# Attention with decay feeding a squared-ReLU MLP in float32: one head pair divided on chip, two more unsplit heads, a third bank, squares on ScalarE

## The chip, the cores and the metric

The kernel runs on one core of a Trainium2 chip. The metric is device time in microseconds (us), the median of repeated executions. The profile is that of a single execution, in which every instruction of the engines has its own record: TensorE (PE, with PEld for its weight loads), VectorE (DVE), ScalarE (ACT), GpSimd (POOL), and SyncE (SP), which here issues most of the DMAs.

## The reference, cut to what matters

```python
# q, k, v: (8, 8, 576, 64), f: (8, 8, 576): 8 batches of 8 heads
scores = scale * q @ k.T
cum = cumsum(log(clip(f, 1e-4, 1.0)), axis=-1)
scores = where(causal, -1e9, scores + cum[..., :, None] - cum[..., None, :])
attn = exp(scores - max(scores))
attn = attn / (sum(attn) + 1e-9)
x = (attn @ v) -> 4608 tokens x 512
h = maximum(x @ w_in, 0.0)          # w_in: 512 x 2048
out = (h * h @ w_out)               # w_out: 2048 x 512
```

The inputs of attention are float32, and w_in and w_out are float64, which the kernel turns to float32 itself, from the two 32-bit words of each number.

## The kernel before, in words

**Heads and slots.** The 64 heads run one after the other, and each is six score units (UNITS), a block of up to 128 keys by a stretch of queries: 320, 320, 192, 64, 448 and 256 queries in this order, the last for the first key block. One unit is one slot, so head h has slots 6h to 6h + 5. In slot n the program writes down, engine by engine: the score products of unit n, the product with v for the unit of two slots earlier (LAG), the steps of a division that are due, the maxima of the next head, preparation and loads of later heads, weight conversion, and steps of the MLP. `in_order` (L18) then keeps each of PE, ACT, DVE and POOL in the order in which this was traced, so a waiting instruction holds all behind it on its engine.

**Precision, and two kinds of head.** Float32 products on PE take two instruction records each and more time than single ones in the rounded type (float32r). Heads below NWHOLE are "unsplit": `score` (L392) and `av_part` (L456) multiply float32 operands as they are, a mask is added in PSUM by a product with the constant mz (L395), and the row of maxima is turned by small products with an identity (`turn_maxima`, L377, L381) and enters the score product as an extra row. From NWHOLE on heads are "split": q, k, v and the probabilities are divided into a rounded high and a low part (`prep` L313 to L324, `split_v` L332 and L333, `split_p` L424 and L425), the products are taken in the rounded type (L399, L402; L435 to L437), POOL masks the probabilities (L411), and the maxima reach the operand by five small DMAs (L359).

**Maxima.** `max_units` (L339): for each stretch of queries one rounded product (L346) into a PSUM bank, then a reduction on DVE (L354) that reads it. The banks come in turn from banks["m"], 4 and 5, until the MLP starts; from then on "m" is empty and the maxima take the score banks, "s". These are 1, 2, 3, then 1, 2, 3, 5 while chunk 0 runs, and 1 and 2 alone from chunk 1's start to chunk 2's.

**Division.** Two heads share a tile of x (heads on partitions 0 to 63 and 64 to 127) and a tile den with the sums of the probabilities, one row a head (L471). `finish` divides a pair in four parts, in batch 0 in the slots 2, 5, 8 and 11 after the pair's last: part 0 sends both rows by DMA into a 128 x 9 tile (L481), part 1 adds epsilon and inverts on DVE (L483, L484) and sends the result to DRAM (L486), part 2 broadcasts it back over 64 partitions each (L489, two DMAs), part 3 multiplies on POOL (L492).

**Weights.** Sixteen pairs of 128 x 512 blocks are converted during the first 97 slots or so by `weight_ops`, a row of 132 small steps on DVE (L228, L233, L236, L240), ACT (L205, L210) and POOL (L216), some per slot by RATES: 1 at first, then 1.6, then 0.8 up to ready[0], then 2.

**MLP.** 18 chunks of 256 tokens by 16 blocks of the hidden layer. Each (chunk, block) is two half-steps: `mlp1`, twelve products (L522) with the two parts of x (`split_x`, L509 and L510) and of the weights, a ReLU (L530), the float32 square g on DVE (L531), the rounded square gh on ACT (L532) and their difference gl on DVE (L533); and `mlp2`, one step behind, six products (L545). A batch's chunks are started when its last pair is divided: ready[0] is slot 60, and `fill` spreads 64 half-steps, chunks 0 and 1, evenly up to ready[1], slot 104. While weights are still being converted, chunk 0 takes a block as soon as its weights are there, and chunk 1 goes on where chunk 0 has to wait (`next_step`).

## Time and profile before

| | |
|---|---|
| median of 3 runs | 1232.01 us (1229.84 to 1234.22) |
| the profiled execution | 1229.0 us |
| its span, first to last instruction | 1227.3 us |
| granted TensorE clock, mean | 0.989 |
| busy PE, PEld, DVE, ACT, POOL | 97%, 85%, 64%, 58%, 31% |

The rows below come from one execution. A group's row has line, engine, operation, tiles and shapes, the count, then busy time and mean of one in ns, and the idle time of the engine just before, with what ended it. A wait's row has who waited for whom, us in total, how often, and the longest. A stage's row has its start and end, its length, busy time (and count) of the engines named, the granted clock, the DMA engines' mean busy share and what they moved. A timeline row has start, length, engine, line and operation. The end of a matmul is modelled, so successive matmuls overlap in the records, and the distance between starts says more than a duration.

### The profile page before, as it was taken

What the parts mean: (1) busy time and instruction counts of PE and PEld (TensorE: products, weight loads), DVE (VectorE), ACT (ScalarE), POOL (GpSimd) and SP (SyncE); (2) the same over time, 40 slices, a digit from 0 to 9 for tenths busy, and PEclk for the clock granted to TensorE, in tenths of its full rate; (3) what the DMA queues carried; (4) which work ended last, traced back from release to release, by engine and by line L of the source; (5) the groups of instructions that cost most, each with busy time, mean ns of one, the idle gap of its engine ahead of it and who ended that gap; (6) DMA issues with size and microseconds to landing.
All of it is one profiled execution on the core that took longest, in us unless ns stands there. A gap on an engine that the chain in (4) does not pass through costs nothing.

```text
span 1227.3 us, 23243 instructions
## 1 busy us (share of the span) xinstructions
PE 1187.9 (97%) x7770; PEld 1047.9 (85%) x7770; DVE 781.5 (64%) x2046; ACT 710.3 (58%) x1748; POOL 376.4 (31%) x566
## 2 busy tenths in 40 slices
PE   6997998899999999999999999999999999999998
PEld 3665877788999899999999989998999899999997
DVE  5767778876666767666665666767666667533322
ACT  2774655556666666665656666666666666533232
POOL 3332234533333333332322243333333433200000
PEclk8998999899999999999999999999999999999999
DMA  7777501121221212111111121211111212000000
GB/s 216 209 187 178 185 16 33 25 70 34 48 50 41 59 41 53 37 44 36 49 19 56 26 59 42 58 41 45 38 52 41 59 41 59 11 28 1 18 18 18
DMA packets 106376, 71.88 MB, mean 59 GB/s; under 512 B 88184, under 2 KB 88184, under 8 KB 106256
## 3 DMA queue, kind: packets, MB, share of 16 engines
q1 hardware_dynamic: 105136, 66.26, 21.0%
q0 software_dynamic: 1120, 4.13, 1.4%
q8 instruction: 62, 1.02, 0.4%
q14 instruction: 58, 0.48, 0.1%
HBM read 60.20 MB, written 9.88 MB: 57 GB/s over the span
## 4 chain that ended last, share of the span: by engine, by line
PE 76%; ACT 2%; issue 2%; POOL 1%; DVE 0%; DVEq 0%; POOLq 0%
PE bank L522 30%; PE bank L545 28%; PE bank L435 3%; PE bank L437 3%; PE bank L402 3%; PE bank L436 3%; PE bank L346 3%; PE bank L399 3%; POOL v L333 0%; ACT den L471 0%; ACT p L409 0%; ACT r L530 0%; ACT ph L424 0%; ACT gh L532 0%; POOL p L411 0%
## 5 line engine op out<-in xcount | busy, mean ns | idle before, releaser
L545 PE MATMUL bank<-w,gh 128*128 128x512 f32 x1152 | 412.9, 399 | 0.0
L522 PE MATMUL bank<-xh,w 128*128 128x256 f32 x2304 | 331.5, 287 | 5.5 <-DVE tcol L354 5.5
L522 PEld LDWEIGHTS bank<-xh,w 128*128 128x128 f32 x2304 | 303.5, 191 | 13.2 <-DVE tcol L354 5.9
L425 DVE TENSOR_TENSOR pl<-p,ph 128x320 fp32r<-128x320 f32 (+4 forms) x300 | 186.0, 620 | 196.9 <-ACT ph L424 191.4
L545 PEld LDWEIGHTS bank<-w,gh 128*128 128x128 f32 x1152 | 217.1, 188 | 38.1
L530 ACT ACTIVATE r<-bank 128x256 f32<-128x256 f32 x288 | 110.3, 383 | 220.3 <-PE bank L522 200.3
L545 PE MATMUL bank<-w,gl 128*128 128x512 f32 x576 | 226.8, 394 | 0.1
L531 DVE TENSOR_TENSOR g<-r 128x256 f32<-128x256 f32 x288 | 128.5, 446 | 139.0 <-ACT r L530 138.3
L411 POOL TENSOR_SCALAR_AFFINE_SELECT p<-p 128x128 f32<-128x128 f32 (+1 forms) x250 | 83.6, 334 | 423.6 <-ACT p L409 322.7
L424 ACT CAST ph<-p 128x320 fp32r<-128x320 f32 (+4 forms) x300 | 124.4, 415 | 152.3 <-POOL p L411 110.2
L522 PE MATMUL bank<-xl,w 128*128 128x256 f32 x1152 | 185.6, 284 | 0.0
L522 PEld LDWEIGHTS bank<-xl,w 128*128 128x128 f32 x1152 | 159.3, 192 | 0.0
L533 DVE TENSOR_TENSOR gl<-g,gh 128x256 fp32r<-128x256 f32 x288 | 134.4, 467 | 35.7 <-DVE g L531 0.9
L409 ACT ACTIVATE p<-bank 128x320 f32<-128x320 f32 (+4 forms) x300 | 115.9, 386 | 62.7 <-PE bank L402 51.2
L354 DVE CUSTOM_DVE_ANT_0 bank<-bank,mz 128x256 f32<-128x256 f32 (+4 forms) x320 | 133.5, 432 | 27.4 <-PE bank L346 23.3
L346 PE MATMUL bank<-rk 66*128 66x320 f32 (+4 forms) x384 | 112.5, 318 | 22.0 <-DVE tcol L354 13.4
L532 ACT ACTIVATE gh<-r 128x256 fp32r<-128x256 f32 x288 | 120.4, 418 | 9.2
L545 PEld LDWEIGHTS bank<-w,gl 128*128 128x128 f32 x576 | 109.0, 189 | 14.3 <-DVE gl L533 0.9
L346 PEld LDWEIGHTS bank<-rk 66*128 66x128 f32 (+1 forms) x384 | 68.2, 182 | 40.1 <-DVE tcol L354 16.5
L435 PE MATMUL bank<-pl,vh 128*65 128x320 f32 (+4 forms) x350 | 97.6, 279 | 4.6 <-ACT den L471 4.6
L436 PE MATMUL bank<-ph,v 128*64 128x320 f32 (+4 forms) x350 | 95.2, 272 | 0.0
L437 PE MATMUL bank<-ph,vh 128*65 128x320 f32 (+4 forms) x350 | 93.8, 274 | 0.0
(85 smaller groups left out, 1523.5 us busy)
## 6 DMA issues: line engine op xcount, KB each, us to landing
qkraw<-in_qk SPq DMA_DIRECT2D x50, 288.0 KB
v<-in_v SPq DMA_DIRECT2D x64, 160.0 KB
den<-rdr SPq DMA_DIRECT2D x64, 144.0 KB
out<-osb SPq DMA_DIRECT2D x36, 256.0 KB
w<-in_w_in SPq DMA_DIRECT2D x16, 512.0 KB
w<-in_w_out SPq DMA_DIRECT2D x16, 512.0 KB
rl<-in_qk SPq DMA_DIRECT2D x14, 288.0 KB
rk<-in_qk POOLq DMA_DIRECT2D x14, 288.0 KB, 5.0
```

The costliest lines, as they stand in the source:

```text
L346: nc.tensor.matmul(ps[:m, :n], st["r2"][:D + 2, q0:q0 + m], st["kl0"][:D + 2, k0:k0 + n], start=True, stop=True,)
L354: nc.vector.tensor_tensor_reduce(out=ps[:m, :n], in0=ps[:m, :n], in1=mz[:m, mo:mo + n], op0=ALU.add, op1=ALU.min, scale=-1.0, scalar=init, ...
L424: nc.scalar.copy(out=ph[:kn, :n], in_=p[:kn, :n])
L425: nc.vector.tensor_tensor(out=pl[:kn, :n], in0=p[:kn, :n], in1=ph[:kn, :n].bitcast(F32), op=ALU.subtract,)
L435: nc.tensor.matmul(acc[:D + 1, o], vh, pl[:kn, i], start=first, stop=False)
L436: nc.tensor.matmul(acc[:D, o], vl, ph[:kn, i], start=False, stop=False)
L437: nc.tensor.matmul(acc[:D + 1, o], vh, ph[:kn, i], start=False, stop=last)
L522: nc.tensor.matmul(ph[:, :T], w[:, s, cc], x[:, cc, :], start=(cc == 0 and k == 0), stop=(cc == NCC - 1 and k == 2),)
L531: nc.vector.tensor_tensor(out=g, in0=r, in1=r, op=ALU.mult)
L532: nc.scalar.activation(out=gh, in_=r, func=AF.Square)
L533: nc.vector.tensor_tensor(out=gl, in0=g, in1=gh.bitcast(F32), op=ALU.subtract)
L545: nc.tensor.matmul(po, g[:, ts], w[:, s], start=(fc == 0 and k == 0), stop=(fc == NF - 1 and k == 2),)
```

## The change

- **Division of heads 6 and 7** (the last pair of batch 0). `finish_here` replaces `finish`. Part 0, in slot 50: for each head five products of a 128-long piece of its den row with a 1.0 put the sums on 128 partitions, in a PSUM bank; DVE adds epsilon and inverts. Part 1, in slot 51: ten products of those columns, broadcast to 64 columns, with an identity spread the inverses over PSUM as den's layout would be; DVE multiplies x by it. No DMA and no POOL is in it. ready[0] becomes slot 53, and x of chunk 0 is split in slot 52 instead of 58; `fill` spreads the same 64 half-steps from slot 53 to 104.
- **NWHOLE 14 to 16**: heads 14 and 15 are unsplit.
- **Bank 7 joins "m"** for the maxima before the MLP starts (the idle products that keep PE awake before slot 0 write to bank 6).
- **The float32 square g** is computed by ACT as long as weights are still being converted, and by DVE after that.
- **The rate of conversion** from ready[0] on is 1.8 steps a slot.

The diff, with some empty lines left out:

```diff
@@ -71,14 +71,14 @@
 
     MAG_LOW, MAG_HIGH = struct.unpack("<2f", struct.pack("<2I", 0x38000000, 0x47EFFFFF))
 
-    NWHOLE = 14
+    NWHOLE = 16
     DEPTH = 4
     cpool = ctx.enter_context(tc.tile_pool(name="cpool", bufs=1))
     wk = ctx.enter_context(tc.tile_pool(name="wk", bufs=2))
     dr = ctx.enter_context(tc.tile_pool(name="dr", bufs=2, space=bass.MemoryType.DRAM))
     psum = ctx.enter_context(tc.tile_pool(name="psum", bufs=1, space=bass.MemoryType.PSUM))
 
-    banks = {"av": [0, 6], "s": [1, 2, 3], "m": [4, 5], "h": [4], "o0": [6], "o1": [7]}
+    banks = {"av": [0, 6], "s": [1, 2, 3], "m": [4, 5, 7], "h": [4], "o0": [6], "o1": [7]}
 
     def bank(use):
 
@@ -475,7 +475,7 @@
         st = state[h]
         den = st["den"]
         if part == 0:
-            st["cmp"] = wk.tile([P, S // D], F32, name="cmp")
+            st["cmp"] = wk.tile([P, 10], F32, name="cmp")[:, :S // D]
 
             for i in range(2):
                 nc.sync.dma_start(out=st["cmp"][i * D:(i + 1) * D], in_=den[i * D:i * D + 1, :])
@@ -492,6 +492,39 @@
             nc.gpsimd.tensor_tensor(out=x, in0=x, in1=den, op=ALU.mult)
             del state[h], state[h - 1]
 
+
+    def finish_here(h, part):
+
+        st = state[h]
+        cuts = [min(j * P, S - P) for j in range(NJ)]
+        if part == 0:
+            one = vhs[0][:, 0, D:D + 1].bitcast(F32)
+            c = st["cmp"] = wk.tile([P, 2 * NJ], F32, name="cmp")
+            for i in range(2):
+                ps = bank("m")
+                for j, q0 in enumerate(cuts):
+                    nc.tensor.matmul(
+                        ps[:, j:j + 1], st["den"][i * D:i * D + 1, q0:q0 + P],
+                        one[i * D:i * D + 1], start=True, stop=True,
+                    )
+                nc.vector.tensor_scalar_add(c[:, i * NJ:(i + 1) * NJ], ps[:, :NJ], EPS)
+            nc.vector.reciprocal(out=c, in_=c)
+        if part == 1:
+            c = st["cmp"]
+            x = xts[h // H][:, (h % H) // 2, :]
+            for a, b in ((0, 512), (512, S)):
+                ps = bank("m")
+                for j, q0 in enumerate(cuts):
+                    if a <= j * P < b:
+                        m = min(S - j * P, P)
+                        for i in range(2):
+                            nc.tensor.matmul(
+                                ps[i * D:(i + 1) * D, j * P - a:j * P - a + m],
+                                c[:, i * NJ + j:i * NJ + j + 1].broadcast_to([P, D]),
+                                eye_r[:, P - m:].bitcast(F32), start=True, stop=True,
+                            )
+                nc.vector.tensor_tensor(out=x[:, a:b], in0=x[:, a:b], in1=ps[:, :b - a], op=ALU.mult)
+            del state[h], state[h - 1]
 
     mst = {}
 
@@ -528,8 +561,11 @@
         gh = wk.tile([P, T], F32R, name="gh")
         gl = wk.tile([P, T], F32R, name="gl")
         nc.scalar.activation(out=r, in_=ph[:, :T], func=AF.Relu)
-        nc.vector.tensor_tensor(out=g, in0=r, in1=r, op=ALU.mult)
+        if len(split_w) == NW:
+            nc.vector.tensor_tensor(out=g, in0=r, in1=r, op=ALU.mult)
         nc.scalar.activation(out=gh, in_=r, func=AF.Square)
+        if len(split_w) < NW:
+            nc.scalar.activation(out=g, in_=r, func=AF.Square)
         nc.vector.tensor_tensor(out=gl, in0=g, in1=gh.bitcast(F32), op=ALU.subtract)
         mst["g", c, fc] = (gh, gl)
 
@@ -591,7 +627,7 @@
 
 
-    RATES = (1, 1.6, 0.8, 2)
+    RATES = (1, 1.6, 0.8, 1.8)
     LAG = 2
     NA = H * NU
 
@@ -618,10 +654,14 @@
         avs.setdefault(n + LAG, []).append((h, u))
     fins = {}
     for h in range(1, NH, 2):
+        if h == H - 1:
+            for part in range(2):
+                fins.setdefault((h + 1) * NU + 2 + part, []).append((finish_here, h, part))
+            continue
         for part in range(4):
-            fins.setdefault(fin(h, part), []).append((h, part))
+            fins.setdefault(fin(h, part), []).append((finish, h, part))
     last_slot = max(fins)
-    ready = [fin(b * H + H - 1, 3) + 2 for b in range(B)]
+    ready = [fin(b * H + H - 1, 3) + 2 if b else H * NU + 5 for b in range(B)]
 
     def fill(n, part):
 
@@ -678,8 +718,8 @@
         if not split:
             at((h - 1) * NU + (4 if h else 3), 0, turn_maxima, h)
     for b in range(B):
-        at(ready[b] - 2, 0, split_x, b * S // T, b + 1)
-    spun = psum.tile([P, 512], F32, name="bank7")
+        at(ready[b] - (2 if b else 1), 0, split_x, b * S // T, b + 1)
+    spun = psum.tile([P, 512], F32, name="bank6")
 
     def spin(n):
 
@@ -716,8 +756,8 @@
             else:
                 av_part(ha, ua, True)
                 av_part(ha, ua - 1, True)
-        for args in fins.get(n, ()):
-            finish(*args)
+        for do, *args in fins.get(n, ()):
+            do(*args)
         for do in events.get((n, 0), ()):
             do()
         wr = RATES[0] * (n < -NU) if n < -NU // 2 else RATES[1 if n < 0 else 2 if n < ready[0] else 3]
```

What PE has written down in slots 50 to 52 before; L392 and L395 are score products, L456 those with v, L346 the maxima of head 9:

```order
L456 MATMUL bank_1044<-ph,v 65x320
L346 MATMUL bank_1046<-rk_80 128x192
L346 MATMUL bank_1056<-rk_80 64x64
L392 MATMUL bank_1059<-rl 66x64
L395 LDWEIGHTS mz
L395 MATMUL bank_1059<-p,mz 66x64
L456 MATMUL bank_1044<-pl,v 65x320
L392 MATMUL bank_1071<-rl 128x448
```

And after, at the same place; den holds the sums, cmp their inverses, vh_83 the 1.0 and p the identity:

```order
L456 MATMUL bank_1041<-ph,v 65x320
L506 MATMUL bank_1044<-vh_83,den 128x1 x5
L506 MATMUL bank_1051<-vh_83,den 128x1 x5
L346 MATMUL bank_1059<-rk_80 128x192
L346 MATMUL bank_1069<-rk_80 64x64
L392 MATMUL bank_1072<-rl 66x64
L395 LDWEIGHTS mz
L395 MATMUL bank_1072<-p,mz 66x64
L456 MATMUL bank_1041<-pl,v 65x320
L521 MATMUL bank_1078<-p,cmp 64x128 x8
L521 MATMUL bank_1088<-p,cmp 64x64 x2
L392 MATMUL bank_1098<-rl 128x448
```

The twenty products stand among the score units; the first product of the MLP (now L555) stands in slot 53 where it stood in slot 60.

VectorE before, from the part of the reductions in slot 56 to the split of x (L509, L510) in slot 58:

```order
L354 ISA bank_1147,p<-bank_1147,mz 128x192
L354 ISA p 128x1
L236 SCALAR_TENSOR_TENSOR osb<-w_847,osb 128x512
L354 ISA bank_1157,p<-bank_1157,mz 64x64
L354 ISA p 64x1
L240 SCALAR_TENSOR_TENSOR osb<-w_847,osb 128x512
L509 CAST xh_1187<-xt_333 128x1024
L510 TENSOR_TENSOR xl_1188<-xt_333,xh_1187 128x1024
```

And after, slots 50 to 52, from the inversion on:

```order
L511 RECIPROCAL cmp<-cmp 128x10
L354 ISA bank_1059,p<-bank_1059,mz 128x192
L354 ISA p 128x1
L233 TENSOR_SCALAR osb<-wmag 128x512
L354 ISA bank_1069,p<-bank_1069,mz 64x64
L354 ISA p 64x1
L526 TENSOR_TENSOR xt_333<-xt_333,bank_1078 128x512
L526 TENSOR_TENSOR xt_333<-xt_333,bank_1088 128x64
L236 SCALAR_TENSOR_TENSOR osb<-w_770,osb 128x512
L542 CAST xh_1113<-xt_333 128x1024
L543 TENSOR_TENSOR xl_1114<-xt_333,xh_1113 128x1024
```

The split of x (now L542, L543) follows VectorE's own multiply (L526) and no longer POOL's. Up to line 494 both kernels have the same line numbers; the MLP's L522, L530 to L533 and L545 are L555, L563 to L569 and L581 after the change.

## The prediction

> **What bounds the kernel now.** I read the page first, then the table by stage, then the waits and the timeline of the early stages, and last the chain. A slot is one score unit, six to a head, and has one exp (L409); slot numbers come from counting those. Up to 93.4 us there are 26 and 25, slots 0 to 50, 1.30 us each:
>
> ```profile
> L409 ACT ACTIVATE ph<-bank x26: 330/436/545, 26.9 to 91.7; 128x320 f32<-128x320 f32 x9, 128x192 f32<-128x192 f32 x9, 128x448 f32<-128x448 f32 x8
> L409 ACT ACTIVATE pl<-bank x25: 219/383/438, 27.7 to 90.2; 128x320 f32<-128x320 f32 x9, 66x64 f32<-66x64 f32 x8, 128x256 f32<-128x256 f32 x8
> ```
>
> The page's head and its TensorE row:
>
> ```profile
> span 1227.3 us, 23243 instructions
> PE   6997998899999999999999999999999999999998
> ```
>
> The TensorE row is full from the ninth slice (30.7 us each) on; its holes lie in the first eight. The table by stage says the same: core time, PE busy (count), PEld, DVE, ACT, POOL, granted clock, DMA share, GB/s.
>
> ```profile
> 26.90:93.40 66.50, 62.97 (x354) 41.35 (x353) 48.48 (x153) 48.59 (x120) 22.26 (x30) 1.00 0.77 202
> 93.40:111.40 18.00, 11.49 (x64) 7.34 (x62) 12.30 (x29) 10.07 (x24) 6.34 (x8) 0.92 0.93 210
> ...
> 115.70:151.30 35.60, 35.27 (x222) 29.31 (x221) 28.67 (x66) 19.32 (x49) 8.84 (x8) 1.00 0.64 200
> 151.30:192.20 40.90, 38.82 (x238) 31.57 (x237) 30.17 (x69) 22.87 (x55) 14.36 (x12) 1.00 0.08 19
> 192.20:240.50 48.30, 41.10 (x246) 36.09 (x245) 41.19 (x87) 27.83 (x68) 24.41 (x27) 0.93 0.13 30
> ...
> 278.70:1080.00 801.30, 798.81 (x5442) 729.30 (x5441) 531.26 (x1437) 505.94 (x1260) 275.35 (x432) 1.00 0.18 44
> ```
>
> From 278.7 us PE is busy for 798.8 of 801.3 us, so nothing there can absorb or return time: what the change moves before that point moves the end by as much (between slot 98 and there the order is the same too, and I leave its waits as they are). The stages are attention alone (slots 0 to 50), the change-over to the MLP (up to the first L522), heads 10 and 11, heads 12 and 13 (unsplit, weights in conversion), and heads 14 and 15 (split, weights in conversion).
>
> **How the sum is made.** From slot 98 on both programs issue the same work, and both have issued 55 half-steps of the MLP by then: 28 of the first layer (12 L522 each) and 27 of the second (6 L545 each). In the profile before, slot 98's exp is the last of the fifteen below, at 247.2 us. First come the exps, then L522 and L545 by stage, then the chain's price of a half-step.
>
> ```profile
> L409 ACT ACTIVATE p<-bank x15: 203/409/546, 192.2 to 247.2; 128x320 f32<-128x320 f32 x6, 128x192 f32<-128x192 f32 x3, 66x64 f32<-66x64 f32 x2, 128x448 f32<-128x448 f32 x2
> ```
>
> ```profile
> 110.00:247.10 137.10, 50.42 (x336) 46.99 (x336) 0.94 0.25 72
> ...
> 115.70:151.30 35.60, 13.31 (x96) 12.12 (x96) 1.00 0.64 200
> 151.30:192.20 40.90, 14.83 (x108) 13.65 (x108) 1.00 0.08 19
> 192.20:240.50 48.30, 16.75 (x108) 16.09 (x108) 0.93 0.13 30
> ```
>
> ```profile
> 110.00:247.10 137.10, 43.22 (x162) 29.10 (x162) 0.94 0.25 72
> ...
> 115.70:151.30 35.60, 12.85 (x48) 8.57 (x48) 1.00 0.64 200
> 151.30:192.20 40.90, 13.18 (x49) 8.99 (x50) 1.00 0.08 19
> 192.20:240.50 48.30, 15.62 (x60) 10.47 (x59) 0.93 0.13 30
> ```
>
> ```profile
> 245.58 1.40 PE bank L545 x6
> ...
> 248.07 1.43 PE bank L522 x12
> ```
>
> Taking the half-steps out of each stage leaves the cost of a slot of attention with whatever PE waits for in it. Heads 10 and 11: 35.6 less 8 x 1.43 and 8 x 1.40 is 13.0 us over 11 slots, 1.18. Heads 12 and 13: 40.9 less 9 x 1.43 and 8.2 x 1.40 is 16.6 over 12, 1.38. Heads 14 and 15: 48.3 less 9 x 1.43 and 10 x 1.40 is 21.4 over 12, 1.78. I take the time of slot 98 after the change from these prices, part by part.
>
> **Third bank for maxima.** The two rows are what the maxima's matmul (L346) waited for in slots 0 to 50.
>
> ```profile
> PEld bank L346 <- DVE p L354: 8.2, 17, 1.1
> ...
> PE bank L346 <- DVE p L354: 3.2, 8, 0.8
> ```
>
> With two banks a maximum's matmul waits for VectorE's reduction two units back, and that one often stands behind a conversion step. With three it waits for the one three back, half a slot more (about 0.65 us) against waits whose longest is 1.1. PE lost at least the 3.2 us and at most the 8.2; that the weight loads waited 17 times and PE only 8 puts the truth between. I take 5 saved, bounds 0 to 8. Next in line is ACT, busy 48.6 of 66.5 us, and the DMA at 0.77. Slots 0 to 52 lasted from 26.9 to 96.1 us (the row of slot 53 is below), 69.2; they become 64.2. The idle matmuls' move from bank 7 to 6 costs nothing: they end before slot 0.
>
> **Division of heads 6 and 7.** The timeline shows the old chain: reciprocal's sum, slot 53's exp, the broadcast from DRAM, the multiply on POOL, the split of x, the first MLP matmul.
>
> ```profile
> 95.84 0.16 DVE L483 TENSOR_SCALAR cmp<-cmp 128x9 f32<-128x9 f32 x1
> ...
> 96.11 0.38 ACT L409 ACTIVATE pl<-bank 128x256 f32<-128x256 f32 x1
> ...
> 99.37 1.11 SPq L489 DMA_DIRECT2D den<-rdr  x2
> ...
> 106.14 1.39 POOL L492 TENSOR_TENSOR xt<-xt,den 128x576 f32<-128x576 f32 x1 [4.05 <-DMA den<-rdr]
> ...
> 107.56 1.79 DVE L509 CAST xh<-xt 128x1024 fp32r<-128x1024 f32 x1 [4.74 <-POOL xt L492]
> ...
> 109.39 1.22 DVE L510 TENSOR_TENSOR xl<-xt,xh 128x1024 fp32r<-128x1024 f32 x1
> ...
> 111.41 2.08 PE L522 MATMUL bank<-xh,w 128*128 128x256 f32 x8 [5.50 <-DVE tcol L354]
> ```
>
> VectorE stood 4.7 us at the head of its queue for POOL, with the next maxima and conversions behind it, and PE then stood 5.5 us. The clock was 0.92 over these 18 us, about 2.9 us at half, and still low after it (the first eight L522 took 2.08 us). I put the loss at 8.5 us: 5.5, about 2 for the half clock, 1 of smaller waits. Removed are five DMAs on SP's queue, the which loads of q, k and v stood behind, and POOL's 1.39 us. Added are PE products and VectorE work. Two float32 pairs of PE, five products of single width, and a conversion step of VectorE give the prices:
>
> ```profile
> 94.77 0.57 PE L377 MATMUL bank<-p 128*65 128x128 f32 x5
> ...
> 98.08 0.59 PE L456 MATMUL bank<-pl,v 128*65 128x256 f32 x2
> 98.51 0.38 PE L456 MATMUL bank<-ph,v 128*65 128x128 f32 x2
> ```
>
> ```profile
> L236 DVE SCALAR_TENSOR_TENSOR osb<-w,osb 128x512 int32<-128x512 int32 x32 | 29.4, 919 | 0.3
> ```
>
> The 256-column pair holds PE from 98.08 to 98.51: 0.43, so 0.22 for 128 columns. L521 is eight such and two halves: 2.0 us. L506 is ten one-column pairs that the trace doesn't show; by L377's 0.11 an instruction they are at most 2.3, by their columns near nothing: 1.2. For the reciprocal PE waits perhaps 0.5. Between the last product and the first L555 VectorE does L526 (576 columns, 0.7 by L510's 1.22 for 1024), the conversion step (0.9), and the split of x (1.8 and 1.2 above): 4.6 us, of which the PE work of slot 52 and half of 53 covers about 2. PE stands some 2.5. Sum with 0.8 for the clock: 7.0, bounds 4 to 11, against 8.5. What is gained besides is that eight slots no longer run without MLP work: the 55 half-steps begin at slot 53, not 60, and none stands behind the idle.
>
> The clock: in the stage of heads 14 and 15 it was 0.93, so 6.8 of 48.3 us at half, though no wait of PE there passed 2.4 us (rows below). So a stand of 2.5 us may halve the clock for some 3.4 us, a loss of 1.7; I charge half of it. The Trainium skill ("TensorE: Matmul & The Clock Gate", "Why this matters for your kernels") would have only gaps over about 3 us do that; by it the 0.8 falls away and the sum is 0.8 lower. This trace disagrees.
>
> **Heads 14 and 15 unsplit.** Waits in their stage before:
>
> ```profile
> POOL p L411 <- ACT p L409: 14.8, 8, 4.2
> ...
> ACT ph L424 <- POOL p L411: 7.0, 5, 3.9
> ...
> PE bank L346 <- DVE tcol L354: 3.7, 3, 2.4
> ...
> PE bank L346 <- DVE rk L314: 2.4, 1, 2.4
> ```
>
> Unsplit, the POOL mask, the casts, the differences and ten column transfers on SP go; PE gets float32 products in place of single ones. The pair just before is unsplit in the same surroundings (conversion, two score banks, a later head's preparation) and took 1.38 a slot against 1.78: 12 x 0.4 = 4.8 us saved, its dearer PE work already in it. Bounds 0 and 7.2 (at 1.18).
>
> **Square on ACT, rate 1.8.** 27 squares leave VectorE and come to ACT. Prices:
>
> ```profile
> L531 DVE TENSOR_TENSOR g<-r 128x256 f32<-128x256 f32 x288 | 128.5, 446 | 139.0 <-ACT r L530 138.3
> ...
> L532 ACT ACTIVATE gh<-r 128x256 fp32r<-128x256 f32 x288 | 120.4, 418 | 9.2
> ```
>
> That is 12.0 us off VectorE and 11.3 onto ACT over some 130 us. ACT is busy 22.9 of 40.9 us in heads 12 and 13, and the second layer runs a whole step later, which covers the longer chain: 0, bounds -4 to +6. The Trainium skill ("ScalarE: Activation LUTs", "Rules for kernel authors") wants products on VectorE and not on ScalarE; by it this edit loses. These rows, at float32, have ACT no slower. The conversion has 132 steps: 58.8 by slot 60 and 2 a slot ended before at slot 96.6; 53.2 by slot 53 and 1.8 a slot end at 96.8. No change.
>
> **Sum.** Slot 53 at 26.9 + 64.2 = 91.1; division 7.0; 55 half-steps 28 x 1.43 + 27 x 1.40 = 77.8; slots 53 to 66 (one chunk) 14 x 1.18 = 16.5; slots 67 to 97 (two chunks, fewer score banks) 31 x 1.38 = 42.8. Slot 98 comes at 235.2 in place of 247.2: 12 us earlier. The profiled execution, 1229.0 us with 1227.3 of span, becomes 1217; the median of the runs stands 3 above it, so 1232 becomes 1220.
>
> **Rivals.** One: the third bank is worth nothing, since VectorE or, at a DMA share of 0.77, late loads hold the slots at 1.3 us. Then 1225. For it: VectorE is busy 48.5 of 66.5 us; against: no wait on a load stands in that stage. Two: the division on chip stalls PE as long as the old one (11 and a slow start of the MLP): 1225 to 1228. Three: both together, or the MLP's half-steps wait for weights just converted because they now start earlier: within 3 us of 1232. Four, slower: ACT becomes late in slots 61 to 97. It has a third activation per first-layer half, its exps free the only two score banks, and PE waits for them. If all 27 squares show (11.3 us), and heads 14 and 15 stay at 1.78 (4.8), -12 becomes +4 to +8 with one or two more clock drops: 1236 to 1240. It decides once ACT is busy over nine tenths there; it was 0.56.
>
> **How the numbers follow.** The forecast has 0.70, with 1212 to 1227 as its own bounds (bank 0 to 8, division 4 to 11, pair 0 to 7). Rival one 0.10, two 0.07, three 0.07, four 0.06. A change under 0.3 percent, 3.7 us, can't be told from none. Faster: 0.70 + 0.10 + most of two = 0.86; same 0.08; slower 0.06. The range, 1209 to 1230, takes in rivals one and two above, and below a case where several terms come out at their good ends.
>
> **What would show it.** Right: the waits of L346 on p L354 in slots 0 to 50 fall under 3 us and slot 53's exp comes near 91; the first L555 starts between 96 and 101; slot 98's exp near 235; the stage of heads 14 and 15 near 1.4 a slot less its half-steps; the rest unchanged. Wrong: slot 53 still near 96 (rival one), a PE stand over 5 us before L555 (two), ACT over nine tenths in slots 67 to 97 with PE waiting for L409 (four), or any shift after slot 98.

## The result, and the profile after

The changed kernel took 1223.94 us (median of 7 runs, 1220.76 to 1228.45) against 1232.55 for the kernel before (7 runs): 0.9932 of it, with a 95% interval of 0.9911 to 0.9953, or 8.4 us less by that ratio. On another chip, that of the last four runs below, it took 1219.48 us, 0.992 (0.9907 to 0.9933) of the kernel before there. The forecast was 1220 with a range of 1209 to 1230.

The profiled execution after is the slowest of its seven, 1228.45 us. The page's head, with the TensorE row and the granted clock in 40 slices:

```profile
span 1226.7 us, 23251 instructions
...
PE   6999999889999999999999999999999999999998
...
PEclk8988999999999999999999999999999999999999
```

Of the holes that the TensorE row had in its first eight slices, those of the fourth and the seventh are gone. The eighth still has one, and the ninth, full before, has a new one. The clock has low slices, the third and the fourth, where the row is full. The table by stage (columns as in the prediction) shows slots 0 to 50, a piece of them, slots 51 to 53, a piece that overlaps that, slots 85 to 97, and the long rest:

```profile
26.90:91.30 64.40, 62.16 (x348) 43.03 (x347) 46.53 (x147) 47.75 (x119) 22.27 (x30) 0.95 0.84 199
71.30:78.10 6.80, 6.80 (x24) 4.76 (x23) 4.99 (x17) 3.25 (x9) 3.82 (x4) 0.50 0.44 100
91.30:100.60 9.30, 9.30 (x65) 6.78 (x63) 6.36 (x19) 2.97 (x8) 1.86 (x2) 0.71 0.86 229
95.20:102.00 6.80, 6.80 (x36) 5.14 (x33) 4.19 (x7) 1.80 (x5) 0.92 (x1) 0.50 0.86 237
194.50:239.00 44.50, 39.14 (x228) 31.53 (x227) 27.75 (x62) 25.08 (x64) 15.06 (x13) 0.96 0.09 22
278.70:1080.00 801.30, 798.26 (x5427) 727.27 (x5426) 532.76 (x1435) 505.28 (x1256) 275.02 (x432) 1.00 0.18 43
```

Two stretches of 6.8 us run at half clock, which cost this execution half of their length, 6.8 us together. The waits of slots 0 to 50, with VectorE's reduction and a load:

```profile
PE bank L392 <- DMA rl<-cum_dr: 1.9, 1, 1.9
...
PEld bank L346 <- DVE p L354: 0.3, 1, 0.3
```

The wait of L346 that was 8.2 us in 17 times is 0.3 us in one. Slot 50 nevertheless came at 91.3 us, as it had before (91.7): 1.9 us went to a late load, and the half clock that followed at 71.3 us cost 3.4. The timeline of TensorE and then of VectorE in the division:

```profile
91.65 1.97 PE L506 MATMUL bank<-vh,den 1*128 1x1 f32 x20
...
94.61 1.71 PE L521 MATMUL bank<-p,cmp 128*64 128x128 f32 x20
...
100.45 0.77 PE L555 MATMUL bank<-xh,w 128*128 128x256 f32 x2
```

```profile
96.22 0.82 DVE L526 TENSOR_TENSOR xt<-xt,bank 128x512 f32<-128x512 f32 x2 [1.36 <-PE bank L521]
...
97.56 0.69 DVE L542 CAST xh<-xt 128x1024 fp32r<-128x1024 f32 x1
98.28 1.23 DVE L543 TENSOR_TENSOR xl<-xt,xh 128x1024 fp32r<-128x1024 f32 x1
```

TensorE has no idle time in brackets anywhere here: the 5.5 us stand ahead of the MLP is gone. Slot 98's exp came at 241.2 us, 6.0 earlier than before. Up to there half clock cost about as much as before: the 6.8 us and 1.8 more in slots 85 to 97 (0.04 of 44.5), against 8.2 (0.06 of 137.1) from 110 us on in the profile before.

The execution on the other chip, with a span of 1217.5 us, shows what is left when the clock holds. Its stages: slots 0 to 50, 51 to 53, 54 to 98, 85 to 97 alone, 99 to 108.

```profile
26.40:86.70 60.30, 59.23 (x347) 40.84 (x346) 46.80 (x149) 47.65 (x118) 22.56 (x30) 1.00 0.88 215
86.70:93.70 7.00, 7.00 (x66) 5.36 (x65) 4.30 (x17) 3.01 (x8) 1.86 (x2) 1.00 0.74 161
93.70:232.60 138.90, 131.14 (x803) 106.27 (x802) 88.76 (x206) 86.73 (x217) 41.05 (x40) 1.00 0.33 94
187.00:230.30 43.30, 37.91 (x230) 30.33 (x228) 28.58 (x62) 25.07 (x63) 15.12 (x13) 1.00 0.10 23
232.60:267.90 35.30, 30.96 (x193) 26.90 (x193) 22.55 (x60) 17.56 (x44) 11.38 (x17) 0.95 0.21 61
```

The clock is 1.00 up to slot 98, which comes at 232.6 us, 14.6 earlier than before and 2.6 earlier than forecast; of the 14.6, some 8.5 is half clock that this execution does not have. But the span is only 9.8 us shorter: between slots 98 and 108, 3.8 us come back. That stretch took 31.5 us before and 35.3 here, of which 1.7 is a new half-clock period (the 0.95). Its row before, a wait of TensorE in it before, and TensorE's waits in it here:

```profile
247.20:278.70 31.50, 29.17 (x196) 25.86 (x195) 22.39 (x59) 17.35 (x45) 12.14 (x17) 1.00 0.24 68
```

```profile
PE bank L346 <- DVE rk L314: 0.2, 1, 0.2
```

```profile
PE bank L346 <- DVE tcol L354: 2.9, 2, 2.2
PE bank L346 <- DVE rk L314: 1.4, 1, 1.4
```

The wait of 2.2 us stood there before too; new are 0.7 for a reduction right after slot 98 and 1.2 more for the preparation of a head (L314). In the first profile the same stretch is 3.8 us longer as well (35.3 us, 241.2 to 276.5), and of the twelve usable profiles of the changed kernel and its variants ten have a half-clock period that begins in it, 20 to 22.5 us after slot 98. So this part of the loss belongs to the change and not to one execution.

### The profile page after: what moved, and what is told of

Read it like the earlier page. It is cut to its first block, busy times and chain, and to the rows that moved or that the text cites. A ratio compares the mean times of both kernels' runs of the same rounds, so it can differ in the third digit from the quotient of the medians.

```text
span 1226.7 us, 23251 instructions
## 1 busy us (share of the span) xinstructions
PE 1195.7 (97%) x7816; PEld 1052.2 (86%) x7816; DVE 756.2 (62%) x2004; ACT 713.7 (58%) x1763; POOL 362.1 (30%) x551
## 5 line engine op out<-in xcount | busy, mean ns | idle before, releaser
L581 PE MATMUL bank<-w,gh 128*128 128x512 f32 x1152 | 413.5, 399 | 0.0
L555 PE MATMUL bank<-xh,w 128*128 128x256 f32 x2304 | 331.0, 286 | 2.2 <-POOL w L216 2.1
L555 PEld LDWEIGHTS bank<-xh,w 128*128 128x128 f32 x2304 | 302.4, 190 | 10.6 <-POOL w L216 2.7
L425 DVE TENSOR_TENSOR pl<-p,ph 128x320 fp32r<-128x320 f32 (+4 forms) x288 | 178.2, 619 | 193.9 <-ACT ph L424 189.5
L581 PEld LDWEIGHTS bank<-w,gh 128*128 128x128 f32 x1152 | 217.2, 189 | 38.3
L563 ACT ACTIVATE r<-bank 128x256 f32<-128x256 f32 x288 | 110.6, 384 | 220.6 <-PE bank L555 186.2
L581 PE MATMUL bank<-w,gl 128*128 128x512 f32 x576 | 226.7, 394 | 0.2 <-DVE gl L569 0.2
L424 ACT CAST ph<-p 128x320 fp32r<-128x320 f32 (+4 forms) x288 | 119.4, 415 | 146.6 <-POOL p L411 104.2
L411 POOL TENSOR_SCALAR_AFFINE_SELECT p<-p 128x128 f32<-128x128 f32 (+1 forms) x240 | 77.5, 323 | 412.9 <-ACT p L409 312.0
L565 DVE TENSOR_TENSOR g<-r 128x256 f32<-128x256 f32 x261 | 112.6, 431 | 122.6 <-ACT r L563 122.2
L555 PE MATMUL bank<-xl,w 128*128 128x256 f32 x1152 | 184.8, 283 | 0.0
L569 DVE TENSOR_TENSOR gl<-g,gh 128x256 fp32r<-128x256 f32 x288 | 131.7, 457 | 78.7 <-ACT g L568 46.8
L555 PEld LDWEIGHTS bank<-xl,w 128*128 128x128 f32 x1152 | 158.6, 191 | 0.0
L354 DVE CUSTOM_DVE_ANT_0 bank<-bank,mz 128x256 f32<-128x256 f32 (+4 forms) x320 | 133.4, 433 | 29.0 <-PE bank L346 27.0
L409 ACT ACTIVATE p<-bank 128x320 f32<-128x320 f32 (+4 forms) x288 | 111.7, 388 | 60.6 <-PE bank L402 49.4
L346 PE MATMUL bank<-rk 66*128 66x320 f32 (+4 forms) x384 | 111.3, 321 | 15.9 <-DVE tcol L354 11.1
L581 PEld LDWEIGHTS bank<-w,gl 128*128 128x128 f32 x576 | 109.0, 189 | 14.3 <-DVE gl L569 0.9
L435 PE MATMUL bank<-pl,vh 128*65 128x320 f32 (+4 forms) x336 | 93.2, 277 | 2.6 <-ACT den L471 2.6
L346 PEld LDWEIGHTS bank<-rk 66*128 66x128 f32 (+1 forms) x384 | 68.0, 184 | 31.2 <-DVE tcol L354 12.6
L436 PE MATMUL bank<-ph,v 128*64 128x320 f32 (+4 forms) x336 | 91.2, 271 | 0.0
L437 PE MATMUL bank<-ph,vh 128*65 128x320 f32 (+4 forms) x336 | 89.3, 272 | 0.0
```

The lines of the kernel that those rows point to most:

```text
L346: nc.tensor.matmul(ps[:m, :n], st["r2"][:D + 2, q0:q0 + m], st["kl0"][:D + 2, k0:k0 + n], start=True, stop=True,)
L354: nc.vector.tensor_tensor_reduce(out=ps[:m, :n], in0=ps[:m, :n], in1=mz[:m, mo:mo + n], op0=ALU.add, op1=ALU.min, scale=-1.0, scalar=init, ...
L409: nc.scalar.activation(out=p[:kn, :n], in_=ps[:kn, :n], func=AF.Exp, scale=SCALE)
L424: nc.scalar.copy(out=ph[:kn, :n], in_=p[:kn, :n])
L425: nc.vector.tensor_tensor(out=pl[:kn, :n], in0=p[:kn, :n], in1=ph[:kn, :n].bitcast(F32), op=ALU.subtract,)
L435: nc.tensor.matmul(acc[:D + 1, o], vh, pl[:kn, i], start=first, stop=False)
```

## The experiments

In the first four runs theory A is the prediction's sum: bank 5, division 1.5 and pair 4.8 saved, the square and the rate nothing, and the half-steps moved at no cost. Its rivals: that a term is worth nothing, or that an edit charged at nothing costs time. All ratios are to the kernel before on the same chip; 0.001 is 1.2 us. The intervals reach 0.0013 to 0.0021 to either side, so a difference of two ratios is uncertain by an estimated 2 to 4 us. The first four ran on one chip, the next four on a second, the last four on a third.

**Without the third bank.**

```diff
-    banks = {... "m": [4, 5, 7], ...}
+    banks = {... "m": [4, 5], ...}
```

> The changed kernel with only banks 4 and 5 for the maxima before the MLP starts, all else as changed. Theory A (the prediction's sum): the bank is worth 5 us, so this kernel stands about 3.5 us below the kernel before in place of 8.6, near 1229, and in its profile the weight loads of L346 wait some 8 us for the reductions (p L354) in slots 0 to 50, with slot 33 near 69.5 us. Theory B (late loads and the clock take the bank's gain back before slot 53): the time is that of the changed kernel, 1224 within 2 us, though the waits on p L354 return. Slot 33 tells the local gain, the time what is left of it.

1226.64 us, 0.9964 (0.9948 to 0.998). Its waits in slots 0 to 50 and their table:

```profile
PEld bank L346 <- DVE p L354: 6.8, 14, 1.1
PE bank L346 <- DVE p L354: 2.8, 7, 0.8
```

```profile
27.10:92.00 64.90, 61.83 (x348) 40.80 (x347) 46.76 (x146) 47.92 (x119) 20.51 (x28) 1.00 0.76 200
```

The old waits are back, and slots 0 to 50 take 64.9 us at full clock against 60.3 with the bank. So the bank is worth 4.6 us where it acts, and 3.9 by the ratios (0.9964 less 0.9932).

**Division through DRAM again, with what belongs to it** (MLP from slot 60, rate 2).

```diff
-        if h == H - 1:
+        if False:
...
-    ready = [fin(b * H + H - 1, 3) + 2 if b else H * NU + 5 for b in range(B)]
+    ready = [fin(b * H + H - 1, 3) + 2 for b in range(B)]
...
-        at(ready[b] - (2 if b else 1), 0, split_x, b * S // T, b + 1)
+        at(ready[b] - 2, 0, split_x, b * S // T, b + 1)
...
-    RATES = (1, 1.6, 0.8, 1.8)
+    RATES = (1, 1.6, 0.8, 2)
```

> The changed kernel with heads 6 and 7 divided in four parts through DRAM as before, ready[0] at slot 60 again, and 2 conversion steps a slot after it, so that the conversion ends at the same slot. Theory A: the division is worth 1.5 us and the earlier start of the MLP nothing more, so about 1225.5. Theory B (the small products cost a drop of the TensorE clock, 6.8 us at half in slots 51 to 53 of the changed kernel): nothing is lost or 1 to 3 us are gained, 1221 to 1224, and the clock is full in slots 50 to 53, with a drop before the first L555 instead. Theory C (the empty eight slots were most of the gain): 5 us or more are lost, 1229 or above.

1215.42 us, 0.9875 (0.9854 to 0.9895): not slower but 5.5 to 7 us faster than the changed kernel, by its two measurements, which all three theories missed. VectorE and TensorE behind the old division's multiply on POOL, and the table of slots 51 to 61:

```profile
100.61 0.69 DVE L542 CAST xh<-xt 128x1024 fp32r<-128x1024 f32 x1 [2.80 <-POOL xt L492]
```

```profile
101.45 1.83 PE L555 MATMUL bank<-xh,w 128*128 128x256 f32 x8 [1.55 <-ACT w L210]
```

```profile
87.00:105.80 18.80, 16.68 (x91) 11.62 (x89) 14.29 (x38) 12.38 (x31) 8.88 (x10) 0.91 0.80 202
```

The same slots in the kernel before:

```profile
91.70:115.70 24.00, 17.05 (x89) 11.68 (x88) 15.04 (x39) 12.21 (x30) 7.64 (x10) 0.86 0.76 171
```

The same DMAs, POOL multiply and split as before now leave TensorE standing 1.55 us, not 5.50, and VectorE 2.80, not 4.74. Slots 51 to 61 take 18.8 us, 1.7 of them lost to half clock; before they took 24.0, 3.4 of them lost to half clock. So most of the loss that I had put down to the division belonged to the state it stood in before. This timeline and the one in the prediction show where the 4 us of standing went. TensorE now starts 0.15 us after the cast of x has ended (101.30); before, the cast ended at 109.35 and TensorE waited 2.06 us more, for the reduction that the row there names (tcol L354), which stood behind the split on VectorE. That part is the third bank's: counted through the program, the last maximum ahead of the MLP is the 89th use of "m", and with banks 4 and 5 in turn it falls on bank 4, which the first product of the MLP needs; with a third bank in the turn it falls on bank 5. Of the rest, 1.1 us is the cast, 0.69 us long in place of 1.79, and 0.9 is the multiply on POOL, which starts 0.7 us before TensorE runs out of work in place of 0.2 after it. Why these two are better is not shown.

**Heads 14 and 15 split again.**

```diff
-    NWHOLE = 16
+    NWHOLE = 14
```

> The changed kernel with NWHOLE 14: heads 14 and 15 are split again. Theory A: 12 slots at 1.78 in place of 1.38 us beside the half-steps, 4.8 us lost, about 1229. Rival: the dearer stage of the split pair came from the conversion at 2 steps a slot and the fuller MLP, and the unsplit pair's own PE work is dearer (two records a product), so 0 to 3 us are gained, 1221 to 1224.

1227.87 us, 0.9974 (0.9958 to 0.9991). Against 0.9932 the pair is worth 5.2 us by the ratios. Its waits of TensorE in slots 85 to 97, and the table:

```profile
PE bank L346 <- DVE tcol L354: 3.3, 2, 2.3
PE bank L399 <- DVE tcol L354: 2.4, 2, 1.2
PE bank L555 <- POOL w L216: 2.1, 1, 2.1
```

```profile
187.00:233.30 46.30, 36.77 (x232) 30.92 (x231) 37.86 (x77) 29.96 (x75) 23.01 (x25) 1.00 0.12 28
```

46.3 us against 43.3 with the pair unsplit: the profiles, both at full clock, show 3.0 of the 5.2. The rest goes with the clock: the mean granted clock of the twelve runs is 0.9865 at the median, against 0.991 and 0.993 in the two measurements of the changed kernel. The last of the three waits is not the pair's, since it is there with the pair unsplit too (below).

**The square always on VectorE.**

```diff
-        if len(split_w) == NW:
+        if True:
...
-        if len(split_w) < NW:
+        if False:
```

> The changed kernel with the float32 square always on VectorE. Theory A: no difference within 2 us, 1224, since neither engine is the late one there. Rival one: VectorE's 12 us come back into the stage where its queue holds the maxima up, and 4 us or more are lost, 1228 or above. Rival two: ACT was made late by the 27 squares, and 3 us or more are gained, 1221 or below.

1218.42 us, 0.9897 (0.988 to 0.9914): the square on ScalarE costs some 4 us by this and the first measurement of the changed kernel, 3 by the second. Slots 54 to 98, and TensorE's two longest waits in slots 85 to 97:

```profile
93.60:230.50 136.90, 130.95 (x803) 106.39 (x802) 101.91 (x233) 79.18 (x189) 41.02 (x40) 1.00 0.33 95
```

```profile
PE bank L555 <- POOL w L216: 1.9, 1, 1.9
PE bank L377 <- ACT ph L409: 1.3, 1, 1.3
```

TensorE is busy for the same 131 us as in the changed kernel (131.14), and the stretch is 2.0 us shorter. VectorE carries 13 us more, and no time is lost by it.

After these four a new theory stood: the early start of the MLP makes later slots thin. The work of the half-steps is the same whenever it is done, so what is done in slots 53 to 59, which were full already (shown below), is missing in slots 85 to 97, where TensorE waits for converted weights, exps and maxima.

**The on-chip division, the MLP still from slot 60.**

```diff
-        r0 = ready[b - 1]
+        r0 = max(ready[b - 1], 60)
```

> The changed kernel with one line of the pacing altered: the half-steps are spread from slot 60 to 104 and not from 53, so slots 53 to 59 are attention alone as before; the division on chip, its place and the conversion stay. Theory A (density: the half-steps that were moved ahead of slot 60 are missing in slots 72 to 97, where PE then stands waiting for the conversion, for exps and for maxima): most of the loss goes, about 1216 to 1218, and slots 84 to 97 cost 1.2 to 1.4 us each beside the half-steps in place of 1.5 to 1.65. Theory B (the division on chip costs it, by its small products or the clock): no gain, 1222 to 1225. Theory C (half-steps waiting for weights just converted): in between, 1219 to 1221, since only the waits of L555 for L216 go, 2 us.

1217.41 us, 0.9899 (0.9878 to 0.9919), as the theory of thin slots had it; slots 85 to 97 cost 1.38 us each beside the half-steps, inside its 1.2 to 1.4. Its slots 54 to 98:

```profile
93.70:229.80 136.10, 130.94 (x802) 106.17 (x803) 87.37 (x206) 87.36 (x218) 40.91 (x40) 1.00 0.34 95
```

**From slot 66, and the square on VectorE.** The line above with 66, and both conditions of the square as before.

> The half-steps spread from slot 66 to 104, and the float32 square on VectorE throughout; the rest as changed. Theory A (density): denser still, so another 1 to 3 us below the kernel with the spread from slot 60, and 1 to 4 us from the square: 1212 to 1215. Theory B: not below 1218, which the square alone gave. A third case: two chunks then reach slot 98 two half-steps late and the gain is given back, 1217 or more.

1217.45 us, 0.9891 (0.9878 to 0.9905). No better than from slot 60, and in the third case's range: by slot 98 it has issued 27 and 26 half-steps where the others have 28 and 27. Its profile has 17 us at half clock around the division, so its early stages say little; in slots 85 to 97, at full clock, TensorE waits 0.2 us.

**Rate 2 alone.**

```diff
-    RATES = (1, 1.6, 0.8, 1.8)
+    RATES = (1, 1.6, 0.8, 2)
```

> The changed kernel with 2 conversion steps a slot from slot 53 on, so that the conversion ends near slot 93 and not 97. Theory C (half-steps wait for weights just converted): 2 to 4 us are gained, 1220 to 1222, and the wait of L555 for L216 near slot 96 goes. Theory A (density): within 2 us of the changed kernel, 1222 to 1226, as the other engines' work per slot grows and PE's does not.

1217.83 us, 0.9889 (0.9872 to 0.9905), a larger gain than either theory had. It is against theory A: with the early start and 2 steps a slot, nothing is left of the loss that can be measured. No profile of it can be set beside the others, so there is no stage to show.

**The bank and the unsplit pair alone**: division through DRAM, start at 60, rate 2, square on VectorE.

> The changed kernel without the division on chip (the division through DRAM, spread from slot 60, 2 steps a slot) and with the square on VectorE throughout: what is left of the change is the third bank and the two unsplit heads. If the square's 4 us are a loss wherever ACT carries it: 1211 to 1213. If they were a loss only in the thin slots of the changed kernel: 1214 to 1217, as the kernel without the division, whose PE already stood only 2 us in slots 84 to 97.

1215.38 us, 0.9884 (0.9869 to 0.9899). These two edits alone are faster than all of them together (0.9932 and 0.992). With the start at 60 the square makes no difference.

**The changed kernel again.**

> The changed kernel once more, as the base for the three others on the same chip. Expected 1222 to 1225 us, 0.993 of the kernel before. If its profile shows half clock at other places than 71.3, 95.2, 235.1 and 262.4 us, those drops are not fixed to an instruction of the program; all theories of where the change's time goes have it unchanged.

1219.48 us, 0.992, with the profile shown above. Between slot 0 and the last microseconds it has half clock once, from 254.7 us on, so the falls of the first profile at 71.3, 95.2 and 235.1 us are not tied to an instruction. The last of them, at 262.4, is 21 us behind slot 98, where this profile has its own at 22 us.

**On-chip division with start and conversion as before.**

```diff
-        r0 = ready[b - 1]
+        r0 = max(ready[b - 1], 60)
...
-    RATES = (1, 1.6, 0.8, 1.8)
+    RATES = (1, 1.6, 0.8, 2)
...
-        wr = ... 2 if n < ready[0] else 3]
+        wr = ... 2 if n < 60 else 3]
```

> The MLP of batch 0 still starts at slot 60 and the conversion runs at 0.8 a slot up to slot 60 and 2 after it, so this differs from the kernel without the division on chip (1215.4 us) by the division alone. Theory A, the division on chip loses no more than the one through DRAM does with the third bank: 1214 to 1216.5, ratio 0.987 to 0.9885. Theory B, its small products and its half clock cost more than the 3.9 us that the one through DRAM loses: 1217 to 1219, ratio 0.989 or 0.990, and the stretch from slot 50 to 53 some 7 us long.

1216.58 us, 0.9899 (0.9886 to 0.9913): theory B by the ratio and by the length of slots 51 to 53, on the border between A and B by the time. Its slots 51 to 53, 51 to 61, 54 to 98, 54 to 60 and 85 to 97, and TensorE's waits in the last:

```profile
87.30:94.20 6.90, 6.90 (x65) 5.18 (x63) 4.20 (x17) 2.92 (x8) 1.86 (x2) 1.00 0.76 229
...
87.30:106.10 18.80, 18.64 (x134) 13.69 (x133) 12.21 (x40) 12.36 (x31) 5.00 (x7) 1.00 0.77 217
...
94.20:228.80 134.60, 130.76 (x802) 106.30 (x803) 83.96 (x205) 86.75 (x216) 40.82 (x40) 1.00 0.34 93
94.20:102.40 8.20, 8.05 (x45) 5.39 (x46) 6.78 (x19) 5.96 (x16) 1.83 (x3) 1.00 0.62 177
181.80:225.80 44.00, 42.27 (x256) 34.35 (x256) 27.95 (x66) 27.79 (x70) 15.63 (x14) 1.00 0.10 23
```

```profile
PE bank L456 <- ACT den L471: 0.8, 1, 0.8
PE bank L346 <- DVE tcol L354: 0.5, 1, 0.5
PE bank L377 <- ACT ph L409: 0.3, 1, 0.3
```

The same waits in the changed kernel on the same chip:

```profile
PE bank L555 <- POOL w L216: 2.1, 1, 2.1
PE bank L377 <- ACT ph L409: 1.5, 1, 1.5
PE bank L346 <- DVE tcol L354: 1.1, 1, 1.1
PE bank L346 <- ACT pl L409: 0.7, 2, 0.5
```

This pair of profiles shows where the time went. From slot 53 to 98 TensorE is busy 131.1 and 130.8 us, and the stretch lasts 138.9 and 134.6: the changed kernel has the same work and 4 us more of standing. In slots 85 to 97 its four waits sum to 5.4 us, all of the idle time there (43.30 less 37.91); here three waits make 1.6. The half-steps in those slots, L555 and then L581, in the changed kernel and here:

```profile
187.00:230.30 43.30, 13.22 (x96) 12.10 (x96) 1.00 0.10 23
...
187.00:230.30 43.30, 12.95 (x49) 8.54 (x48) 1.00 0.10 23
```

```profile
181.80:225.80 44.00, 15.36 (x111) 14.29 (x112) 1.00 0.10 23
...
181.80:225.80 44.00, 16.01 (x60) 10.55 (x60) 1.00 0.10 23
```

Eight and eight half-steps against nine and ten, in nearly the same time: the thirteen slots last some 44 us either way. The pair differs in the rate as well as in the start, so it does not part the two; each of them alone, and the square alone, brought the time to 0.989 or 0.990.

**The same with the square on VectorE.**

> As the kernel with start and conversion of before, and the square on VectorE throughout. Theory A, the square costs only where slots have little else for PE, as they had with the early start: within 1 us of that kernel. Theory B, the square on ScalarE costs its 4 us wherever it stands: 1211 to 1213, ratio 0.984 to 0.986.

1216.14 us, 0.9891 (0.9878 to 0.9904), within 1 us: theory A. Its slots 54 to 98:

```profile
94.50:229.80 135.30, 130.81 (x802) 106.28 (x803) 99.59 (x232) 79.20 (x190) 42.41 (x40) 1.00 0.35 93
```

135.3 us against 134.6 with the square on ScalarE. This kernel differs from the kernel with the bank and the pair alone (0.9884) only by the on-chip division, which is worth nothing that can be measured.

**Dense products between the one-column ones.**

```diff
                         one[i * D:i * D + 1], start=True, stop=True,
                     )
+                    nc.tensor.matmul(ps[:, 64:], mz[:, :P], mz, start=True, stop=True)
```

> The changed kernel with a dense product of 448 columns into the unused part of the bank behind each of the ten one-column products, about 2 us of PE work more. Theory A, the half clock from 95.2 us on follows from the twenty small products, which leave TensorE with little to do though it is never idle: it goes, 3.4 us are saved against 2 spent, 1221 to 1223 with a mean granted clock higher by 0.003. Theory B, the drop has nothing to do with them: it stays, and the time is 1225 to 1226.

1226.48 us, 0.9978 (0.9962 to 0.9994). TensorE around the fall of the clock (in this kernel L510 is the added product):

```profile
91.65 0.36 PE L510 MATMUL bank<-mz 128*128 128x448 bf16 x1
...
92.45 0.56 PE L510 MATMUL bank<-mz 128*128 128x448 bf16 x1
```

The added product takes 0.36 us and the next one 0.56: the clock halved at 91.9 us in the middle of them. Theory A is wrong: the dense products did not keep it up here, and the mean granted clock of the twelve runs, 0.990 at the median, is not above the changed kernel's 0.993. The time is 7 us above that of the changed kernel on this chip, where B had 2: VectorE waited for the last of the products with the reciprocal, and slots 51 to 53 took 13.8 us, 3.4 of them lost to half clock.

## Why the prediction was right, and which of its steps were not

The direction, the time and the range held; the time held because steps of the sum were off in opposite directions, and in part by luck with the clock, of which it had only a charge. With the half clock taken out, an estimate from the granted clock of the rows, slot 98 comes 6 us earlier in both profiles (6.0 with as much half clock as before; 14.6 less 8.5 with none), where the sum had 12, and 3.8 come back by slot 108. The runs gained more than that, and they spent less time at half clock: on the second of the two chips the mean granted clock is 0.993 at the median, against 0.987 for the kernel before.

**What bounds it: right, but for the end.** The time came from before slot 108, and the long rest is as busy as it was (798.3 of 801.3 us). That nothing would shift after slot 98 was wrong by 3.8 us, in both profiles: 1.7 is a half-clock period, and 1.9 are two waits of L346, for a reduction and for the preparation of a head.

**Third bank: right.** Forecast 5; measured 4.6 in its stage and 3.9 by the ratios. In the first profile the late load and the half clock in slots 33 to 50 hid this. That is what rival one had named, late loads, but of the twelve usable profiles of the changed kernel and its variants only two have one that holds TensorE there, of 1.9 and 1.1 us.

**Division, "I put the loss at 8.5 us" and 7.0 for the new one: both too large.** L506 took 1.97 us where 1.2 was forecast, L521 1.21 at full clock (1.71 in the first profile, part of it at half) for 2.0, and the stand of 2.5 us did not come: VectorE's multiply and split lay beside slots 52 and 53. At full clock slots 51 to 53 take 7.0 us against 3.6 at 1.21 a slot, a loss of 3.4. But the old division loses no more once it stands in the new surroundings, its half clock counted (1.7 us, and none on chip): slots 51 to 61 take 18.8 us with either (87.0 to 105.8 through DRAM, 87.3 to 106.1 on chip with start and conversion as before). So the step that failed is the attribution of 5.5 us of standing and of the half clock behind it to the division. I read it as the price of the DMAs and of POOL. 2.06 of the 5.50 us were the wait for bank 4, which the third bank takes away by itself, and all but 1.55 went with the new surroundings.

**"The 55 half-steps begin at slot 53, not 60, and none stands behind the idle": wrong.** The sum let them move at no cost. There was no room: in the kernel with start and conversion as before, TensorE is busy for 8.05 of 8.20 us in slots 54 to 60 with attention alone. The room was in slots 85 to 97, and the early start took the work away that had covered its waits. What that costs depends on the two edits below: with the square on ScalarE and 1.8 steps a slot it is 3 to 4 us, and with 2 steps a slot nothing that can be measured. Of the 5.4 us of waits there, 2.1 are rival three's mechanism, half-steps that wait for weights just converted; the others, for exps and maxima, are in no rival.

**Square on ACT and rate 1.8, both "0": a part of the same loss.** The square alone put back saves 2.0 us from slot 53 to 98, the late start alone 2.8, start and rate together 4.3, all three 3.6. They do not add: that each relieves the same waits, for an exp and for a weight just converted, fits them, but no run parts these waits. With the late start the square is free, as forecast. The rule of the Trainium skill ("ScalarE: Activation LUTs", "Rules for kernel authors") that products belong on VectorE agrees in direction with the runs with the early start (3 to 4 us) and not with those with the late one (nothing), at about the same duration of the square (0.40 us on ScalarE, 0.43 on VectorE, in the profile of the changed kernel). That it matters only where TensorE waits for ScalarE's queue fits this, but is argued.

**Heads 14 and 15: right in size, in part by luck.** Forecast 4.8; 5.2 by the ratios, 3.0 between two profiles at full clock. The price of 1.78 came from a stage with 6.8 of its 48.3 us at half clock, so 3.4 of the 4.8 us were half clock and not work or waits: at full clock the same sum gives 1.4. The measured 5.2 holds half clock too (0.9865 against 0.991 and 0.993); why the split heads have more of it is not shown. The price of 1.38 a slot was not met with the early start: 43.3 us less 8 x 1.43 and 8 x 1.40 is 20.7 for 13 slots, 1.59. With start and conversion as before it was: 44.0 less 9.3 x 1.43 and 10 x 1.40 is 16.7, or 1.28.

**The clock: half right.** A charge of 0.8 us was too small for the first profile, which lost 3.4 us at the division, and too large for the second, which lost nothing there. The spread of the changed kernel goes with the clock: the seven runs of the first measurement go from 1220.76 us at a mean granted clock of 0.993 to 1228.45 at 0.987.

Put together, the bank and the unsplit pair carry the gain (0.9884 alone), the division on chip adds nothing to it, and the early start, the square and the rate give 3.5 to 5 us back (0.992 and 0.9932 against 0.9891). The kernel with these two edits, at 1215.4 us, beats both kernels, and no run here beats it clearly.

## What to carry to other kernels

Before work is moved earlier, ask which slots have room for it and which need it as cover: moved out of a stretch where the engine waits into one where it is full, it gains nothing and can uncover the waits. A stall that the trace puts at one chain of transfers belongs to the state that the chain stands in, so when another edit changes that state, price the stall again before paying for its removal. Of a change of several edits, make those that stand alone first, and keep each of the others only if it still gains with them.

## What the runs showed of the hardware

TensorE's clock halved without any idle time of TensorE in the 10 us ahead of it: at 95.2 us in the first profile, 3.6 us after the first one-column product (91.65), and 3.6 us after it again in the kernel with dense products in between (88.3 to 91.9). Of the ten usable profiles with these products four have a fall within 3.6 us of the first of them; the second profile of the changed kernel has none. The Trainium skill ("TensorE: Matmul & The Clock Gate", "What's actually happening") has a free-running window of 3.4 us by which the clock is set, so that the same program can meet it differently from run to run. The lengths here agree, 3.4, 6.8 and 10.2 us, and the spread between executions fits it. The other rule of the Trainium skill, that gaps over some 3 us bring the fall ("Why this matters for your kernels"), does not cover a fall with no gap, nor one behind a shorter stand, such as that of 1.55 us in the kernel divided through DRAM; what the small products share with idleness was not found.

Ten one-column float32 products, two records each, held TensorE 1.97 us, 0.1 us a record, about as much as a record of L377 with 128 columns (0.57 us for five): between these rows the columns cost next to nothing, and a product was not made cheap by having one column.
